# Local attention by quarter blocks of 32 queries, with the scores of three items in one piece on TensorE

## The chip, the cores and the metric

The kernel runs on one core of a Trainium2 chip. The time is device microseconds of that core for one launch. Before the change it is 918.82 us, the median of three runs (917.39 to 920.97).

## The reference, cut to what matters

Attention over 4 batches and 8 heads of width 64, then two feed-forward layers on the result. Each head has 32 global tokens and 512 local ones.

```python
window = 32
s_g = scale * np.matmul(q_g, k_all.transpose(0, 1, 3, 2))          # 32 global queries see all 544 keys
out_g = np.matmul(sm(s_g), v_all)
mask = np.abs(pos[:, None] - pos[None, :]) <= window               # a local query sees keys up to 32 away
s_ll = np.where(mask, scale * np.matmul(q_l, k_l.transpose(0, 1, 3, 2)), -1e9)
s_l = np.concatenate([scale * np.matmul(q_l, k_g.transpose(0, 1, 3, 2)), s_ll], axis=-1)   # and all 32 global keys
out_l = np.matmul(sm(s_l), np.concatenate([v_g, v_l], axis=2))
x = concat([out_g, out_l]).transpose(0, 2, 1, 3).reshape(B * S, H * D)     # 2176 tokens x 512
h = x @ w_in                                                       # 512 -> 2048
x = np.where(h >= 1, h, np.where(h <= -1, 0, (h + 1) ** 2 / 4)) @ w_out    # 2048 -> 512
return (x @ w_a * (x @ w_b)) @ w_out2                              # 512 -> 1536 -> 512
```

`sm` is a softmax over the last axis with the row maximum subtracted and 1e-9 added to the sum. All is float32; the weights arrive as float64 and are converted on the chip.

## The kernel before, in words

**Tiles.** The 16 blocks of 128 local queries and the block of global queries form six tiles of tokens (`TILES`, line 45): five of three blocks, 384 columns, and one of block 15 and the global block, 256 columns. The two layers work tile by tile. A unit of the first feed-forward layer (`h_unit`, line 767, and `x_unit`, line 796) takes 128 of the 2048 inner columns: 12 matmuls into a bank `hp`, the activation on ScalarE and VectorE, and 12 matmuls into four banks `acc`. Each product of the layers is three matmuls in the float32r format (`mm3`, line 438: high by high, low by high, high by low). After about 460 us the second layer follows; it has no attention in it.

**Attention.** An item (`Local`) is one block of 128 queries and one pair of heads; the two heads lie in the upper and lower 64 partitions. It is split into halves of 64 queries, each with 160 keys: a window of 128 and the 32 global ones. `s_pe` makes the scores with four float32 matmuls on 64x64 tiles of the array, into one bank a head. `s_post` adds the mask and takes the row's extreme in one VectorE instruction a head (line 193), then the exponential and its row sum on ScalarE (line 197). `norm` divides. `t_pe` and `t_post` transpose 320 columns in three overlapping transposes of 128 and copy the result to SBUF. `v_pe` runs once for a group, the items of a tile with one pair of heads (three, in tile 5 one): per item and head one matmul of 128 columns for the global keys and two of 64 columns for the halves, float32, on 128x64 tiles. `Glob` does the same for the global queries of one batch and four heads.

**Order.** `att_atoms` (line 351) is a generator that cuts this work into pieces. In step k it makes the scores of item k, normalises item k-1, transposes item k-2, and, when item k-3 ends a group, makes that group's products; scores and products then form one piece (`joined`). So a group of three has six pieces: three transposes, two scores, one of scores with products. Tile 0's pieces run first, alone, with a step of weight conversion (`W1.step`) after each eight. Then the pieces of tile t+1 are spread evenly over the `h_unit`s and `x_unit`s of the layer on tile t (`credit`, lines 863 to 910): tile 1 over tile 0's first six units, tile 2 over 26 units, tiles 3 and 4 over 16 each, tile 5 with the global items over the first 14 of tile 4. During the units of tiles 0 and 1 the float64 weights are converted: a raw tile of 512 KB lands (two buffers), line 105 on ScalarE and 106, 107 on VectorE make float32 of it, 114 and 115 split it in high and low. `paced` puts such a step behind the activation of the unit just issued.

The framework turns this into one fixed list for each engine. It plans by the order of the program, but takes an instruction ahead when an earlier one isn't ready by its estimate: in the trace the first matmuls of `hp` start at 31.02 us, ahead of tile 0's last transposes at 32.00. It also inserts all waits. PSUM has eight banks in two sets of four. In the set `h` lie scores, `hp` and, from tile 1 on, transposes and results; in the set `acc` the four accumulators and, for tile 0, transposes and results. DMAs are issued almost all from SP's queue, in order.

Of the kernel before, what the change touches and what calls it, by code (L numbers as in the profile page):

```python
# [9 lines left out]
F32 = mybir.dt.float32  # L10
# [8 lines left out]
P = 128  # L19
# [7 lines left out]
HQ = P // 2  # L27
KW = HQ + 2 * WIN + SG
QK = P + 2 * KW
C_ROW = (0, 2 * KW - P, KW - HQ)  # L30
# [18 lines left out]
NWARM, WARM_ITEMS = 2, 12  # L49
NCOLD = 3  # L50
FA = 6
START_ATOMS = 8
# [11 lines left out]
EBUFS = 3  # L64
PTBUFS = 3
VBUFS = 4


def body(tc, qk, vw, kg, vg, w1i, w1o, w2a, w2b, w2o, mask, eye, out):
# [13 lines left out]
    masks = ap.tile([P, 3, SG + KW], BF16, name="masks", bufs=1)  # L83
# [67 lines left out]
    class Local:  # L151
        def __init__(self, t, j, blk, p):
            self.t, self.j, self.p = t, j, p
            self.tag = "h" if t else "acc"
            self.blk = blk
            self.b, self.i = divmod(blk, SL // P)

        def load(self):
            n = nat["n"]
            nat["n"] += 1  # L160
            if 4 <= n < 4 + EARLY:
                self.qk = mp.tile([P, QK], F32, name="qk", tag="g", bufs=3)
            else:
                self.qk = gp["k"].tile([P, QK], F32, name="qk", tag="qk", bufs=4)
# [3 lines left out]
        def load_v(self):  # L168
            self.v = ap.tile([P, 3, P], F32, name="v", bufs=VBUFS)
            nc.sync.dma_start(self.v, vw[self.blk, self.p])  # L170

        def s_pe(self):
            self.s = [ps.tile([P, KW], F32, name=f"s{h}", tag="h") for h in range(2)]
            for a in range(2):
                for h in range(2):
                    r = slice(64 * h, 64 * h + 64)
                    c = slice(HQ * a, HQ * a + HQ)
                    nc.tensor.matmul(self.s[h][c], self.qk[r, c], self.qk[r, P + KW * a:P + KW * (a + 1)],
                                     start=True, stop=True, tile_position=(64 * h, HQ * a))

        def fill(self):
            w = ps.tile([P, 512], F32, name="warm", tag="acc")
            for _ in range(NWARM):
                nc.tensor.matmul(w[:, :P], ident, ident, start=True, stop=True)

        def s_post(self):
            m = 1 if self.i == 0 else (2 if self.i == SL // P - 1 else 0)
            self.ef = ap.tile([P, 2 * KW], F32, name="e", tag="e", bufs=EBUFS)
            self.e = self.ef.rearrange("p (h k) -> p h k", k=KW)
            mn = ap.tile([P, 2], F32, name="mn", tag="mn", bufs=EBUFS)  # L190
# [1013 lines left out]
```

## Time and profile before

| | before |
|---|---|
| median of 3 runs | 918.82 us (917.39 to 920.97) |
| the profiled execution | 920.25 us, its span 918.4 us |
| TensorE busy, granted clock | 904.6 us (98%), 1.000 |
| VectorE busy | 643.0 us (70%) |
| ScalarE busy | 508.5 us (55%) |
| DMA | 153.32 MB, mean 167 GB/s |

The span runs from the first to the last instruction. A busy TensorE is not TensorE at its peak, as its matmuls overlap in the record; what a piece costs is read from how far it moves the matmuls behind it. The granted clock of 1.000 is the upper of its two levels, 2.4 GHz.

### The profile page before, as it was taken

Reading aid. Unit: us, or ns where it says so; the run is one execution under the profiler, and the core shown is the slowest. Engines: PE = TensorE matmul, PEld = TensorE weight load, DVE = VectorE, ACT = ScalarE, POOL = GpSimd, SP = SyncE. Lnnn points to the kernel's source line nnn. Section 1 sums busy time; section 2 is a strip of 40 time slices with the busy share of each in tenths; the row PEclk is TensorE's granted clock in tenths of the full one; section 3 lists DMA queues with packets and bytes.
Section 4 is the critical chain, followed back from the end, with each engine's and each line's share of the span. In section 5 each row is a group of like instructions: output and inputs, shape, how many; then the busy total and the mean of one; then the engine's idle time right before and its main releaser. Section 6 shows DMA issues by size and latency. Waiting matters only on the chain.

```text
span 918.4 us, 17966 instructions
## 1 busy us (share of the span) xinstructions
PE 904.6 (98%) x6606; PEld 832.5 (91%) x6606; DVE 643.0 (70%) x1648; ACT 508.5 (55%) x1227; POOL 0.3 (0%) x5
## 2 busy tenths in 40 slices
PE   9999999999999999999999999999999999999998
PEld 6778998999999999887899999999998999999998
DVE  5888897676556555644478787777887658766683
ACT  7978675555455555534446465554655546555442
POOL 0000000000000000000000000000000000000000
PEclk9999999999999999999999999999999999999999
DMA  8986665765443444344354364443598530643431
GB/s 273 313 240 209 194 223 187 245 198 166 144 138 125 160 126 130 109 124 155 108 195 136 95 207 162 160 142 110 189 307 284 184 93 23 187 158 121 170 135 53
DMA packets 82025, 153.32 MB, mean 167 GB/s; under 512 B 9360, under 2 KB 48400, under 8 KB 81936
## 3 DMA queue, kind: packets, MB, share of 16 engines
q1 hardware_dynamic: 81360, 151.49, 51.1%
q8 instruction: 52, 0.85, 0.4%
q10 hardware_dynamic: 576, 0.67, 0.2%
q14 instruction: 37, 0.30, 0.1%
HBM read 118.83 MB, written 33.29 MB: 166 GB/s over the span
## 4 chain that ended last, share of the span: by engine, by line
PE 81%; DMA 9%; DVE 6%; ACT 2%; issue 1%; SPq 0%; ACTq 0%; DVEq 0%
PE acc L439 6%; PE hp L439 6%; PE hp L441 5%; PE acc L440 5%; PE acc L441 5%; PE hp L440 5%; PE pb L639 4%; PE pb L641 4%; PE pb L642 4%; PE py L706 3%; PE px L639 3%; PE px L641 3%; PE px L642 3%; PE py L707 3%; PE py L705 3%; DMA wraw<-in_w1o_dram 3%
## 5 line engine op out<-in xcount | busy, mean ns | idle before, releaser
L439 PE MATMUL hp<-xh,w 128*128 128x384 f32 (+1 forms) x384 | 130.8, 341 | 2.7 <-DVE m L787 1.6
L439 PE MATMUL acc<-g,w 128*128 128x384 f32 (+1 forms) x384 | 131.1, 341 | 0.0
L440 PE MATMUL acc<-g,w 128*128 128x384 f32 (+1 forms) x384 | 126.8, 330 | 0.0
L441 PE MATMUL acc<-g,w 128*128 128x384 f32 (+1 forms) x384 | 126.1, 328 | 0.0
L441 PE MATMUL hp<-xl,w 128*128 128x384 f32 (+1 forms) x384 | 125.9, 328 | 0.0
L440 PE MATMUL hp<-xh,w 128*128 128x384 f32 (+1 forms) x384 | 125.5, 327 | 0.0
L787 DVE SCALAR_TENSOR_TENSOR m<-hp,r 128x384 f32<-128x384 f32 (+1 forms) x96 | 51.2, 534 | 100.5 <-ACT r L786 100.3
L786 ACT ACTIVATE r<-hp,half 128x384 f32<-128x384 f32 (+1 forms) x96 | 53.8, 560 | 71.3 <-PE hp L441 69.6
L639 PE MATMUL pb<-w 128*128 128x384 f32 (+1 forms) x240 | 78.1, 325 | 1.5 <-DVE m L683 0.8
L439 PEld LDWEIGHTS hp<-xh,w 128*128 128x128 f32 x384 | 72.4, 188 | 7.3 <-DVE m L787 1.7
L114 ACT ACTIVATE w<-wt 128x512 fp32r<-128x512 f32 (+1 forms) x94 | 53.8, 572 | 45.1 <-PE pb L642 28.0
L641 PE MATMUL pb<-w 128*128 128x384 f32 (+1 forms) x240 | 78.2, 326 | 0.0
L642 PE MATMUL pb<-w 128*128 128x384 f32 (+1 forms) x240 | 78.0, 325 | 0.0
L439 PEld LDWEIGHTS acc<-g,w 128*128 128x128 f32 x384 | 72.4, 188 | 5.3 <-issue 4.3
L440 PEld LDWEIGHTS acc<-g,w 128*128 128x128 f32 x384 | 72.6, 189 | 1.4 <-issue 1.3
L441 PEld LDWEIGHTS hp<-xl,w 128*128 128x128 f32 x384 | 72.3, 188 | 1.0 <-DMA xl<-x0d 0.6
L441 PEld LDWEIGHTS acc<-g,w 128*128 128x128 f32 x384 | 72.4, 189 | 0.3 <-issue 0.2
L440 PEld LDWEIGHTS hp<-xh,w 128*128 128x128 f32 x384 | 72.5, 189 | 0.0
L791 ACT ACTIVATE g<-m 128x384 fp32r<-128x384 f32 (+1 forms) x96 | 48.3, 503 | 42.4 <-DVE m L788 42.1
L197 ACT ACTIVATE e<-e,mn 128x160 f32<-128x160 f32 x128 | 53.7, 421 | 26.6 <-DVE mn L193 26.6
L792 DVE TENSOR_TENSOR g<-m,g 128x384 fp32r<-128x384 f32 (+1 forms) x96 | 51.2, 533 | 20.1 <-ACT g L791 19.9
L115 DVE TENSOR_TENSOR w<-wt,w 128x512 fp32r<-128x512 f32 (+1 forms) x94 | 57.9, 616 | 2.7 <-ACT w L114 1.6
(168 smaller groups left out, 2133.1 us busy)
## 6 DMA issues: line engine op xcount, KB each, us to landing
qk<-in_qk_dram SPq DMA_DIRECT2D x62, 224.0 KB, 3.6
wt<-wd SPq DMA_DIRECT2D x50, 256.0 KB, 2.9
v<-in_vw_dram SPq DMA_DIRECT2D x64, 192.0 KB, 4.2
wraw<-in_w1i_dram SPq DMA_DIRECT2D x16, 512.0 KB, 4.3
wraw<-in_w1o_dram SPq DMA_DIRECT2D x16, 512.0 KB, 4.4
wraw<-in_w2a_dram SPq DMA_DIRECT2D x12, 512.0 KB, 3.9
wraw<-in_w2b_dram SPq DMA_DIRECT2D x12, 512.0 KB, 4.0
wd<-wt SPq DMA_DIRECT2D x24, 256.0 KB, 2.1
```

The lines of the kernel that those rows point to most:

```text
L114: nc.scalar.activation(hi, src, AF.Copy)
L115: nc.vector.tensor_tensor(lo, src, f32(hi), ALU.subtract)
L197: nc.scalar.activation(self.e[:, h], self.e[:, h], AF.Exp, bias=mn[:, h:h + 1], scale=-1.0, accum_out=self.sm[:, h:h + 1])
L439: nc.tensor.matmul(acc, whi, xhi, start=first, stop=False)
L440: nc.tensor.matmul(acc, wlo, xhi, start=False, stop=False)
L441: nc.tensor.matmul(acc, whi, xlo, start=False, stop=last)
L639: nc.tensor.matmul(out[:, :n], w[:, 0, r], hi[:, c, :n], start=start and c == 0, stop=False, skip_group_check=True)
L641: nc.tensor.matmul(out[:, :n], w[:, 1, r], hi[:, c, :n], start=False, stop=False, skip_group_check=True)
L642: nc.tensor.matmul(out[:, :n], w[:, 0, r], lo[:, c, :n], start=False, stop=k in (1, 5, 6) and c == 1, skip_group_check=True)
L786: at["act"] = nc.scalar.activation(r[:, :W], hp[:, :W], AF.Relu, bias=half, scale=0.5 / W_UP).ins
L787: nc.vector.scalar_tensor_tensor(m[:, :W], hp[:, :W], 1.0 / W_UP, r[:, :W], ALU.mult, ALU.max)
L792: nc.vector.tensor_tensor(gl[:, :W], m[:, :W], f32(gh[:, :W]), ALU.subtract)
```

## The change

An item is split into quarters of 32 queries, each with 128 keys. For that the keys of a block are laid out as seven slots of 32: the keys from 32 before the block to 64 into it, the 32 global keys, and the keys from 64 in the block to 32 behind it (`SLOTS`). Quarter a uses the four slots from a on; each such run holds its window of 96 and the global keys. Scores are then eight matmuls of 128 columns on 64x32 tiles, two transposes take the place of three, and the products are eight matmuls of 32 columns an item, each with 128 values of its own, on 128x64 tiles. Per item the queries and keys take 176 KB (224 before) and the values 256 KB (192 before).

The pieces are made anew. `groups` holds lists of items: three, or in tile 5 two; the global items count as groups of one. A group's scores are one piece, together with the products of the group two before it; ahead of it the group between is normalised. Each item's transposes are one piece. A group of three so has four pieces instead of six, 16 a tile instead of 24. Loads are asked for in each piece, at most one of each kind, as far as buffers allow (five tiles each). In tile 0 the row sum moves from ScalarE's exponential to one VectorE sum a group, three pieces have four fill matmuls each (nine had two each before), and a step of weight conversion comes after each five pieces. Result banks of tile 0 stay in `acc`.

```diff
-HQ = P // 2
-KW = HQ + 2 * WIN + SG
-QK = P + 2 * KW
+NQ = P // WIN
+SLOTS = (0, 1, 2, None, 3, 4, 5)
+QK = P + WIN * len(SLOTS)
-NWARM, WARM_ITEMS = 2, 12
-NCOLD = 3
+NWARM = 4
+START_GROUPS = 4
+EARLY_END = 13
-START_ATOMS = 8
+START_ATOMS = 5
-EBUFS = 3
+QKBUFS = 5
+EBUFS = 2
-VBUFS = 4
+VBUFS = 5
...
         def s_pe(self):
-            self.s = [ps.tile([P, KW], F32, name=f"s{h}", tag="h") for h in range(2)]
-            for a in range(2):
-                for h in range(2):
...
+            self.s = [ps.tile([P, self.nt, P], F32, name=f"s{h}", tag="h") for h in range(2)]
+            for n, it in enumerate(self.items):
+                for a in range(NQ):
                     for h in range(2):
                         r = slice(64 * h, 64 * h + 64)
+                        c = slice(WIN * a, WIN * a + WIN)
+                        nc.tensor.matmul(self.s[h][c, n], it.qk[r, c], it.qk[r, P + WIN * a:2 * P + WIN * a],
+                                         start=True, stop=True, tile_position=(64 * h, WIN * a))
+
+        def s_post(self):
...
+            for n, it in enumerate(self.items):
+                m = 1 if it.i == 0 else (2 if it.i == SL // P - 1 else 0)
+                for h in range(2):
+                    nc.vector.tensor_tensor_reduce(
+                        self.e[:, n, h], self.s[h][:, n], masks[:, m], -SCALE, 3.0e38, ALU.add, ALU.min,
+                        mn[:, n, h:h + 1])
+                for h in range(2):
+                    acc = self.sm[:, n, h:h + 1] if self.t else None
+                    nc.scalar.activation(self.e[:, n, h], self.e[:, n, h], AF.Exp, bias=mn[:, n, h:h + 1],
+                                         scale=-1.0, accum_out=acc)
+
+        def norm(self):
+            sm = self.sm[:, :self.nt]
+            if not self.t:
+                nc.vector.tensor_reduce(sm, self.e[:, :self.nt], mybir.AxisListType.X, ALU.add)
+            nc.vector.tensor_scalar_add(sm, sm, 1e-9)
+            nc.vector.reciprocal(sm, sm)
+            for n in range(self.nt):
+                nc.scalar.activation(self.e[:, n, 0], self.e[:, n, 0], AF.Copy, scale=self.sm[:, n, 0:1])
+                nc.vector.tensor_scalar_mul(self.e[:, n, 1], self.e[:, n, 1], self.sm[:, n, 1:2])
+
+        def t_pe(self, n):
+            it = self.items[n]
+            tp = ps.tile([P, 2, P], F32, name="tp", tag=self.tag)
+            for h in range(2):
+                nc.tensor.transpose(tp[:, h], self.e[:, n, h], ident)
+            it.pt = ap.tile([P, 2, P], F32, name="pt", tag="pt", bufs=PTBUFS)
+            nc.scalar.activation(it.pt, tp, AF.Copy)
+
+        def v_pe(self):
+            self.o = ps.tile([P, self.nt * P], F32, name="o", tag=self.tag)
+            for n, it in enumerate(self.items):
+                for a in range(NQ):
+                    for h in range(2):
+                        r = slice(64 * h, 64 * h + 64)
+                        q0 = WIN * a
+                        nc.tensor.matmul(self.o[r, n * P + q0:n * P + q0 + WIN], it.v[:, a, r],
+                                         it.pt[:, h, q0:q0 + WIN], start=True, stop=True)
...
+    def may_k():
+        n = ld["k"]
...
+        return n < ld["s_done"] + (8 if n < EARLY_END else QKBUFS)
...
+    def loads(first):
+        for may, fn in ((may_k, load_k), (may_v, load_v)):
+            k = 0
+            while may() and (k < 1 or (first and fn is load_k)):
+                fn()
+                k += 1
...
+    def piece(gs, gv):
+        def run():
+            loads(gs == 0)
+            if gs is not None:
+                if gs > START_GROUPS:
+                    groups[gs - 1].norm()
+                s_part(groups[gs])
+            if gv is not None:
+                v_part(groups[gv])
+            if 0 < (gs or 0) < START_GROUPS:
+                fill()
+            if gv is not None:
+                groups[gv].v_post()
+                if groups[gv].t == 0:
+                    x_chunk(0, groups[gv].items[0].p, widths(0))
+            if gs is not None:
+                groups[gs].s_post()
+        return run
+
+    def tpose(g, n):
+        def run():
+            loads(False)
+            if n == 0 and (g < START_GROUPS or g == len(groups) - 1):
+                groups[g].norm()
+            groups[g].t_pe(n)
+        return run
+
+    atoms = [piece(0, None), piece(1, None)]
     ends = {}
+    ns = 2
+    for g, grp in enumerate(groups):
+        n = grp.nt if isinstance(grp, Local) else 1
+        atoms += [tpose(g, i) for i in range(n)]
+        hold = g == START_GROUPS - 2
+        atoms.append(piece(None if hold or ns >= len(groups) else ns, g))
+        ns += not hold
+        if grp.t >= 0:
+            ends[grp.t] = len(atoms)
+        if g == START_GROUPS - 1:
+            atoms.append(piece(ns, None))
+            ns += 1
...
-                    n_atoms = sum(2 + it.last - joined(k + 3) for k, it in enumerate(todo, done["n"]))
+                    n_atoms = ends[goal[si]] - done["n"]
                     rate = n_atoms / (2.0 * (GLOB_END if t == nt - 2 else n_units) - 1)
```

For the global items the values load into the same buffers as the local ones, their last 32 rows as a tile of their own, and the copy of their transposes is two instructions instead of one.

## Rows read from the trace of the kernel before

**Rows 1.** Stretches: busy us of PE, PEld, DVE, ACT, POOL; clock, DMA, GB/s.

```profile
4.00:31.10 27.10, 25.69 (x298) 18.52 (x298) 19.36 (x102) 23.28 (x82) 0.00 (x0) 1.00 0.91 301
31.10:85.00 53.90, 50.31 (x468) 40.46 (x469) 46.23 (x164) 44.46 (x129) 0.00 (x0) 1.00 0.83 261
85.00:160.00 75.00, 73.00 (x511) 68.30 (x509) 63.84 (x157) 50.74 (x114) 0.00 (x0) 1.00 0.61 194
160.00:380.00 220.00, 219.92 (x1689) 203.72 (x1689) 134.17 (x403) 116.42 (x298) 0.00 (x0) 1.00 0.49 157
```

**Rows 2.** Chain of waits, 37:67 us: by line, then pieces (start, us).

```profile
by line: DMA wraw<-in_w1i_dram 63.0%; DVE wt L107 10.6%; ACT wt L105 8.0%; issue 6.8%; DVE w L115 4.4%; ACT w L114 2.1%; DVE m L788 1.8%; DVE wt L106 1.7%; DVE xl L330 1.6%; DVE sm L202 0.5%; DVE sm L201 0.3%; SPq L97 0.2%; DVE xraw L232 0.
...
38.05 5.60 DMA wraw<-in_w1i_dram
45.94 3.72 DMA wraw<-in_w1i_dram
```

**Rows 3.** Chain of waits, 85 to 150 us, by line.

```profile
by line: DMA wraw<-in_w1o_dram 39.3%; DVE wt L107 12.5%; ACT wt L105 6.3%; DVE wt L106 6.1%; DVE w L115 6.0%; DVE m L787 5.1%; DVE m L788 3.7%; issue 3.5%; DVE g L792 3.3%; PE hp L439 2.3%; ACT w L114 1.8%; DVE e L193 1.8%; PE hp L440 1.6%;
```

**Rows 4.** Chain of waits, 165 to 380 us, by line.

```profile
by line: PE acc L439 14.7%; PE hp L439 14.6%; PE hp L440 13.5%; PE hp L441 13.4%; PE acc L441 13.4%; PE acc L440 13.3%; PE s L178 5.8%; PE tp L209 4.3%; PE o L221 3.8%; PE o L227 3.2%
```

**Rows 5.** TensorE timeline round a scores piece: start us, us, what.

```profile
222.18 0.33 PE L440 MATMUL acc<-g,w 128*128 128x384 f32 x1
222.36 0.34 PE L441 MATMUL acc<-g,w 128*128 128x384 f32 x1
222.62 0.50 PE L178 MATMUL s<-qk 64*64 64x160 f32 x8
...
223.34 0.34 PE L440 MATMUL hp<-xh,w 128*128 128x384 f32 x1
```

**Rows 6.** TensorE's timeline behind a transposing piece.

```profile
225.28 0.49 PE L209 MATMUL tp<-ident,e 128*128 128x128 f32 x3
...
225.78 0.34 PE L440 MATMUL acc<-g,w 128*128 128x384 f32 x1
```

**Rows 7.** TensorE's timeline round a piece of scores and products.

```profile
354.42 0.34 PE L441 MATMUL acc<-g,w 128*128 128x384 f32 x1
354.69 0.50 PE L178 MATMUL s<-qk 64*64 64x160 f32 x8
355.12 0.44 PE L221 MATMUL o<-pt,v 128*64 128x128 f32 x4
355.39 0.40 PE L227 MATMUL o<-pt,v 128*64 128x64 f32 x8
355.62 0.39 PE L221 MATMUL o<-pt,v 128*64 128x128 f32 x4
...
356.08 0.39 PE L221 MATMUL o<-pt,v 128*64 128x128 f32 x4
...
356.63 0.45 PE L439 MATMUL hp<-xh,w 128*128 128x384 f32 x1
356.91 0.34 PE L440 MATMUL hp<-xh,w 128*128 128x384 f32 x1
```

**Rows 8.** TensorE's timeline, a global item's scores, then products.

```profile
388.60 1.12 PE L261 MATMUL sg<-kg 64*32 64x272 f32 x16
389.65 0.44 PE L221 MATMUL o<-pt,v 128*64 128x128 f32 x4
```

**Rows 9.** ScalarE's groups, 4 to 31.1 us: count, busy us, mean ns, idle before.

```profile
L197 ACT ACTIVATION_READ_ACCUMULATOR e<-e,mn 128x1 f32 x26 | 4.9, 189 | 0.0
L213 ACT ACTIVATE pt<-tp 128x384 f32<-128x384 f32 x10 | 4.8, 478 | 0.6 <-PE tp L209 0.6
```

**Rows 10.** VectorE's groups, 380 to 460 us.

```profile
L271 DVE TENSOR_REDUCE mng<-sg 128x1 f32<-128x272 f32 x16 | 6.8, 435 | 1.8 <-PE sg L261 1.6
```

**Rows 11.** VectorE's groups, 4 to 31.1 us.

```profile
L193 DVE CUSTOM_DVE_ANT_0 e<-s,masks 128x160 f32<-128x160 f32 x27 | 7.8, 320 | 9.0 <-PE s L178 5.0 <-PE tp L209 2.0 <-ACT pt L213 1.7
```

More of the change, by code (lines that the diff above doesn't have):

```diff
@@ L168, in load_v @@
         def load_v(self):
[L169 removed]
+            self.v = ap.tile([P, NQ, P], F32, name="v", tag="v", bufs=VBUFS)
             nc.sync.dma_start(self.v, vw[self.blk, self.p])
[L172 to L179 removed]
@@ L181, in fill @@
[L181 to L190, printed above, removed]
-            self.sm = ap.tile([P, 2], F32, name="sm", tag="sm", bufs=EBUFS)
-            for h in range(2):
-                nc.vector.tensor_tensor_reduce(
-                    self.e[:, h], self.s[h], masks[:, m, SG - SG * h:SG - SG * h + KW], -SCALE, 3.0e38,
-                    ALU.add, ALU.min, mn[:, h:h + 1])
-            for h in range(2):
-                nc.scalar.activation(self.e[:, h], self.e[:, h], AF.Exp, bias=mn[:, h:h + 1],
-                                     scale=-1.0, accum_out=self.sm[:, h:h + 1])
@@ L211, in t_post, with fill @@
[L211 to L223 removed]
+    def fill():
+        w = ps.tile([P, 512], F32, name="warm", tag="acc")
+        for _ in range(NWARM):
+            nc.tensor.matmul(w[:, :P], ident, ident, start=True, stop=True)
@@ L234, in body @@
+        def v_post(self):
+            runs = []
+            for n, it in enumerate(self.items):
+                if runs and runs[-1][0].p == it.p:
+                    runs[-1][2] += 1
+                else:
+                    runs.append([it, n, 1])
+            for it, n, w in runs:
+                nc.vector.tensor_copy(xraw_cur[self.t][it.p][:, it.j * P:(it.j + w) * P],
+                                      self.o[:, n * P:(n + w) * P])
     class Glob:
-        last = True
         t = -1
+        nt = 1
@@ L394, in body @@
-    att = att_atoms()
+    groups = []
+    for t, blks in enumerate(TILES):
+        loc = [(j, blk) for j, blk in enumerate(blks) if blk != GLOB]
+        its = [Item(j, blk, p) for p in range(NPAIR) for j, blk in loc]
+        n = len(loc) if len(loc) > 1 else 2
+        groups += [Local(t, its[i:i + n]) for i in range(0, len(its), n)]
+        for b in GSCHED.get(t, []):
+            groups += [Glob(b, q) for q in range(2)]
+    ld = {"k": 0, "v": 0, "s_done": 0, "v_done": 0, "vb": 0, "g": 0}
@@ new lines, in body, with load_k, load_v @@
+    flat_items = [(g, it) for g in groups for it in g.items]
+    first_glob = next(n for n, (g, it) in enumerate(flat_items) if isinstance(g, Glob))
+    started = set()
+    def load_k():
+        n = ld["k"]
+        g, it = flat_items[n]
+        it.load()
+        ld["k"] += 1
+        if n == 0:
+            nc.scalar.dma_start(masks, mask)
+        elif n == 3:
+            nc.scalar.dma_start(ident, eye)
+    def load_v():
+        g, it = flat_items[ld["v"]]
+        it.load_v()
+        ld["v"] += 1
+        ld["vb"] += 1 + isinstance(g, Glob)
```

231 lines of the change are left out of this document (88 added, 143 removed).

## The prediction

> **What bounds the kernel now.** I read the table of stretches first, to see where TensorE has slack, then the chain of waits of each stretch, to see what sets the pace there, then TensorE's timeline around single pieces of attention, for their prices, and last the groups of instructions of the start.
>
> The table of stretches [rows 1] shows four regimes. From 4 to 31 us tile 0's attention runs alone; ScalarE is busy 23.28 of 27.10 us. From 31 to 85 us tile 1's attention runs beside six units of the first layer and the conversion of their weights; TensorE, VectorE and ScalarE are busy for 82 to 93%. From 160 to 380 us TensorE is busy 219.92 of 220.00 us, VectorE 134.17. The chains say what that means. From 37 to 67 us 63% of the chain is the landing of a weight tile, 3.7 to 5.6 us each, then conversion, then the next tile into the freed buffer [rows 2]: TensorE isn't the bound there. From 85 to 150 us the same loop and VectorE's part of it hold most of the chain and matmuls are a small part [rows 3]. From 165 to 380 us the chain is all TensorE [rows 4]: there a microsecond of TensorE is a microsecond of the kernel, and all of what follows after 460 us is only shifted.
>
> **What a group of three items costs TensorE now.** One main matmul starts 0.17 us after the other [rows 5]. A transposing piece moves the second main matmul behind it from 225.28 + 0.17 to 225.78 [rows 6]: 0.33 us for three transposes, 0.11 each, with no cost at the borders. A scores piece on its own: from 222.36 to 223.34, less two main matmuls, 0.63 us [rows 5]. A scores piece with the products of a group: from 354.42 to 356.91, less two, 2.14 us [rows 7]. A group has three of the first, two of the second, one of the third: 0.99 + 1.26 + 2.14 = 4.39 us.
>
> **The change, part by part.** *Transposes:* two for three, 3 x 0.22 = 0.66 us; saves 0.33.
>
> *Scores:* three items in one piece, so two of three entries and exits go. What stands: 0.27 us from the last main matmul to the first score [rows 7], and 0.28 us at the end from the first main matmul to the second [rows 7]. Between them the passes (a float32 matmul leaves two records, one a pass; the eight records of a scores piece lie within 0.50 us [rows 5], so matmuls on different tiles of the array run side by side, and eight records are two passes). Two passes of 160 columns with what surrounds them take 0.43 us [rows 7], four of 272 columns 1.05 us [rows 8]; the difference, 0.62 us for 768 columns, is 0.81 ns a column, and 0.17 us is left for entry and drain. Six passes of 128 columns: 0.62 + 0.17 = 0.79 us. This takes eight tiles of 64x32 to run together; the trace has four of them [rows 8] and four of 64x64, which fill the array [rows 5]. If only four ran at once it would be 1.41 us. I take 0.79, because the whole array is in use there [rows 5].
>
> *Products:* the columns that stream for an item fall from 2 x 128 + 4 x 64 to 8 x 32, the two heads side by side. But each of the 24 passes (3 items, 4 quarters, 2) loads its own 128x64 weights. Before, four passes of 64 columns take 0.23 us (355.39 to 355.62) [rows 7], 0.057 each. No row has a pass of 32 columns. Below, half of that, 0.029, if the product alone counts; above, 0.086, if the load and the product follow each other. I take 0.057, the nearest row: the first pair of passes after the switch takes 0.27 us where a later pair takes about 0.23 (0.46 from 355.62 to 356.08 less 0.23), so 0.04 us is a bare weight load, more than 32 columns would hide. Then 24 x 0.057 = 1.37, with 1.51 - 3 x 0.46 = 0.13 around it [rows 7]: 1.50 us, against 1.51 now. The halved columns buy nothing.
>
> Two rules of the Trainium skill part here. "TensorE: Matmul & The Clock Gate", section LDWEIGHTS, has a load take P/1.2 ns for P columns whatever the rows: 53 ns for these 64, and the products stay at 1.50 us; the 0.04 and 0.057 us above agree with it. "TensorEngine Tiling (Array Packing)", section Instruction Overhead, has a matmul of few columns cost about 60 cycles, 25 ns as an estimate: by that alone a group's products take some 0.7 us. No run here shows a 32-column pass yet; the second is the first rival below.
>
> The piece: 0.27 + 0.79 + 1.50 + 0.28 - 0.35 = 2.49 us; the group 0.66 + 2.49 = 3.15 us; 1.24 us saved in each group, nearly all from borders and transposes.
>
> *Where it counts.* (a) Tiles 3 and 4 and the second half of tile 2, after 150 us, ten groups: 12.4 us. (b) Tile 5's four single items become two groups of two; by the same prices (two transposing pieces of 0.22 and 0.27 + 0.58 + 1.04 + 0.28 - 0.35 = 1.82 a group, against four items at 0.33 + 0.43 + 0.59 and borders, some of them shared with the global items) about 1.5 us. (c) Tile 2's first two groups lie beside the weight loop [rows 3]: between 0 and 2.5, I take 1.2. (d) Tile 1's four groups: up to 5.0, but for half of that stretch the weight loop sets the pace [rows 2] and none of it is touched; I take 2.5. (e) The start. 24 reads of the accumulator, 0.19 us each [rows 9], go, as tile 0 now sums on VectorE; the copy of transposes shrinks from 384 columns to 256. Both together relieve ScalarE by up to 7 us. Against this VectorE gets a sum over 768 elements a group: 272 elements take 0.435 us [rows 10], so at most 1.2 us, 4.9 for four groups. It has 7.7 us free [rows 1]. The first reductions now also wait for three items' loads, and 12 fill matmuls stand where 18 did: the granted clock of the start is 1.00, 2.4 GHz [rows 1], and some us at 1.2 GHz would cost as many. So from -2 to +7; I take 3.
>
> *Edits that I cost at nothing.* Masking, exponentials and normalisation of 128 columns instead of 160 on engines that are off the path after 160 us (VectorE has 86 us free there [rows 1]); in the early stretches their relief, some 0.3 us an item, is inside (c) to (e). Bytes: 176 KB + 256 KB an item for 224 + 192; 4% more on a DMA that is 49% busy after 160 us and 83 to 91% before 85 us [rows 1]; there it can lengthen the landings of weight tiles [rows 2], inside the bounds of (d) and (e). Loads move from fixed steps to each small step, at most one of each kind a step; they queue on SP beside the weight tiles, and with five buffers of each kind a group's three tiles are asked for one to three steps ahead. The global items keep their matmuls; their copy becomes two. Two buffers for the exponentials instead of three hold a group each, so two groups live where three items did.
>
> Sum: 12.4 + 1.5 + 1.2 + 2.5 + 3 = 20.6 us. The profiled execution took 920.25 us, 1.85 outside the span: it would become 899.7. It is 0.16% above the median of the runs, 918.82, so the predicted median is 898.2 us. What is late next is the weight loop before 150 us, and TensorE still after it.
>
> **Rivals.** *First: the products' passes do shorten* to 0.029 us. For it: the load overlaps the running product in every row. Against: the bare load of 0.04 us. It would take 24 x 0.028 = 0.67 us more off each group, eight or so more for (a) and (b): 890.
>
> *Second: the load and the product of a short pass follow each other*, 0.086 us. For it: no row has a load longer than its product. Against: passes of 64 columns run at the length of their product. 0.70 us back per group: 906.
>
> *Third: the early stretches give nothing* because the weight loop carries on as it is and the start trades ScalarE's relief for VectorE's sums and for waits in a batch of three. For it: the loop's share of the chains [rows 2, 3]. Against: ScalarE's 86% in the start [rows 1]. (c) to (e) fall away: 905. The eight tiles running four at a time, so that the change doesn't do what it says, adds 0.62 us to each group and lands there too, 906.
>
> *Fourth, slower: the scores hold their banks.* Scores, transposes, results and the first layer's sums share four banks of PSUM. A group now keeps two until VectorE has gone through six reductions, 0.32 us each now [rows 11], 1.9 us, in a queue with everything else. Where VectorE has 39% free (160 to 380 us [rows 1]) they may take 4.9 us. Cover is the products, 1.5 us, and one unit of 12 main matmuls, 2.1 us. The rest, 1.3 us in 12 pieces, is 15.6; before 160 us, with VectorE 85% busy, say 3 us in six pieces, 18: 918.8 - 20.6 + 33.6 = 932. It decides from 20.6/18 = 1.15 us a piece. Against it: the reductions of an item need no more than its scores and can run under the products.
>
> **Chances.** The forecast 0.58, in a range of its own from 892 to 905; first rival 0.12; second 0.10; third 0.15; fourth 0.05. The range of 8 in 10 takes the two middle rivals in and most of the first: 888 to 908. Half a per cent (4.6 us) is about what a measurement can tell from no change: faster by over that 0.92, within it 0.04 (the second and third rival together, or a mild fourth), slower 0.04.
>
> **What would show it.** In the profile after, a transposing piece moves the main matmul by 0.22 us; a joint piece costs 2.5 us, its 48 product records a row of 1.4 us and its scores 0.6 to 0.8; from 160 us the chain is still TensorE alone, and VectorE's idle time isn't seen ahead of its matmuls. The last stage, after the attention, keeps its 458 us. The forecast is wrong if the joint piece is far from 2.5 us, if first-layer matmuls wait for VectorE after 160 us, or if the first of them starts later than 31 us.

## The result and the profile after

The changed kernel takes 905.95 us, median of four runs (905.32 to 906.93), against 919.89 us in four runs of the kernel before (917.39 to 923.74): a ratio of 0.985 (95% interval 0.981 to 0.988). The forecast was 898.2 us with a range of 888 to 908, so the time lies inside the range and 7.75 us above the forecast. The profiled execution took 905.32 us, with a span of 903.5 us.

| | before | after |
|---|---|---|
| span of the profiled execution | 918.4 us | 903.5 us |
| TensorE busy | 904.6 us | 887.1 us |
| mean granted clock | 1.000 | 0.987 |
| VectorE, ScalarE busy | 643.0, 508.5 us | 634.3, 489.1 us |

The clock is the line to stop at. The first fence is the page's row of the granted clock of the kernel after, 40 slices of 22.6 us; before, all 40 digits were 9.

```profile
PEclk8799999999999999999999999999999999999999
```

The table of stretches of the same execution shows where: the same four stretches as [rows 1], with the same columns.

```profile
4.00:31.10 27.10, 23.27 (x384) 17.09 (x384) 15.48 (x76) 15.77 (x46) 0.00 (x0) 0.81 0.78 254
31.10:85.00 53.90, 48.13 (x637) 40.11 (x635) 44.07 (x149) 42.29 (x132) 0.00 (x0) 0.87 0.82 269
85.00:160.00 75.00, 74.78 (x635) 72.87 (x635) 66.58 (x169) 53.57 (x131) 0.00 (x0) 1.00 0.69 216
160.00:380.00 220.00, 219.69 (x2097) 212.28 (x2097) 133.47 (x375) 112.33 (x304) 0.00 (x0) 1.00 0.49 158
```

In the start ScalarE and VectorE are busy for 15.8 and 15.5 us of 27.1, where they were for 23.3 and 19.4: over the whole stretch neither of them is the bound any more. But the granted clock is 0.81 and 0.87 up to 85 us, and 1.00 behind it. Cut finer, it has only the two levels:

```profile
10.00:14.00 4.00, 1.24 (x49) 0.78 (x48) 2.75 (x9) 1.45 (x5) 0.00 (x0) 1.00 1.00 379
14.00:24.25 10.25, 10.13 (x133) 7.52 (x117) 4.93 (x21) 5.78 (x16) 0.00 (x0) 0.50 0.55 165
24.25:34.50 10.25, 9.30 (x182) 7.07 (x180) 8.11 (x30) 7.76 (x21) 0.00 (x0) 1.00 0.79 257
34.50:48.10 13.60, 11.95 (x90) 10.02 (x90) 7.13 (x29) 7.89 (x26) 0.00 (x0) 0.50 0.80 278
48.10:85.00 36.90, 33.73 (x482) 28.17 (x481) 33.54 (x114) 31.92 (x101) 0.00 (x0) 1.00 0.82 269
```

For 10.25 + 13.60 = 23.85 us TensorE runs at 1.2 GHz, and it is busy for 10.13 + 11.95 = 22.08 us of them. If that work took half as long at 2.4 GHz, 11.0 us would be saved; that is the most that the lower level can have cost here. Ahead of the first fall TensorE worked 1.24 us in 4.

TensorE's timeline of the kernel after shows what it waited for (start, us, what; in brackets the idle time before it and what ended it):

```profile
10.11 0.86 PE L190 MATMUL s<-qk 64*32 64x128 f32 x32
13.73 0.51 PE L190 MATMUL s<-qk 64*32 64x128 f32 x16 [2.76 <-DMA qk<-in_qk_dram]
14.17 0.69 PE L222 MATMUL tp<-ident,e 128*128 128x128 f32 x2
...
31.41 1.59 PE L233 MATMUL o<-pt,v 128*64 128x32 f32 x48
...
34.43 0.67 PE L500 MATMUL hp<-xh,w 128*128 128x384 f32 x1 [0.86 <-ACT xh L340]
...
37.38 1.54 PE L222 MATMUL tp<-ident,e 128*128 128x128 f32 x6 [1.65 <-ACT e L215]
38.85 2.78 PE L233 MATMUL o<-pt,v 128*64 128x32 f32 x48
...
43.70 0.52 PE L500 MATMUL hp<-xh,w 128*128 128x384 f32 x1
44.02 0.52 PE L501 MATMUL hp<-xh,w 128*128 128x384 f32 x1
```

At 10.11 us the scores of group 2 start; two items go through, and the third waits 2.76 us for its load. The transposes of group 0 stand behind it in TensorE's fixed order. The second fall, at 34.5 us, has a wait of 0.86 us ahead of it and one of 1.65 us inside it. The price of the lower level can be read in two places: the 48 product records of a group take 1.59 us at 31.41 and 2.78 us at 38.85, 1.75 times as long; and one main matmul starts 0.32 us after the other (43.70, 44.02) instead of 0.17 [rows 5], 1.85 times. By these factors the 22.08 us hold 9.5 to 10.1 us more than at 2.4 GHz, an estimate.

A second reading is when the k-th main matmul starts (the matmuls of the first layer, counted in the traces from zero). It is the same work in both kernels, so differences between columns are what each stretch gained:

| k | 0 | 72 | 144 | 432 | 1520 | 1900 | end |
|---|---|---|---|---|---|---|---|
| before, us | 31.0 | 55.6 | 83.5 | 144.2 | 379.3 | 475.7 | 918.4 |
| after, less before | -2.3 | +9.5 | +5.6 | +1.5 | -10.6 | -15.6 | -14.9 |

The start loses 9.5 us up to the 72nd, and every stretch behind it up to the 1900th gains: 3.9, 4.1, 12.1 and 5.0 us. The loss isn't the clock alone. Here is all that stands ahead of the 72nd main matmul, first before the change, then after it, with the columns of [rows 1]:

```profile
0.00:55.57 55.57, 51.23 (x512) 39.75 (x512) 40.74 (x174) 44.43 (x135) 0.30 (x5) 1.00 0.88 287
0.00:65.06 65.06, 55.38 (x737) 43.62 (x737) 41.61 (x165) 41.68 (x123) 0.30 (x5) 0.82 0.76 250
```

TensorE stands idle for 9.7 us instead of 4.3, 5.3 more. The lower clock makes its work 9.5 to 11.0 us longer (the estimates above), and what is left over, 5.3 to 6.8 us, is work that fell away. One place of the waiting is the 2.76 us above. Another shows in the chain of waits:

```profile
27.85 0.56 DVE xraw L244
...
36.94 0.40 ACT e L215
37.38 1.54 PE tp L222 x6
```

From 27.85 to 36.94 us it runs over VectorE, busy for 9.04 of these 9.09 us, where normalisation, one of the new row sums (0.86 us), copies, the next scores' reductions and weight conversion stand in one queue, then over ScalarE; the granted clock there is 1.00 up to 34.5 us.

The first layer itself runs to 530.5 us before the change and to 514.9 after it, so the second layer doesn't follow at about 460 us, as the description of the kernel before has it: what ends there (459.0 us) is the attention.

In the steady stretch the pieces can be read as in [rows 6, 7]: first a transposing piece, then a group's scores with the products, both between main matmuls.

```profile
340.63 0.34 PE L502 MATMUL acc<-g,w 128*128 128x384 f32 x1
340.80 0.38 PE L222 MATMUL tp<-ident,e 128*128 128x128 f32 x2
...
341.20 0.34 PE L501 MATMUL hp<-xh,w 128*128 128x384 f32 x1
```

```profile
224.98 0.34 PE L502 MATMUL acc<-g,w 128*128 128x384 f32 x1
225.25 0.94 PE L190 MATMUL s<-qk 64*32 64x128 f32 x48
226.12 1.59 PE L233 MATMUL o<-pt,v 128*64 128x32 f32 x48
227.64 0.44 PE L500 MATMUL hp<-xh,w 128*128 128x384 f32 x1
227.92 0.34 PE L501 MATMUL hp<-xh,w 128*128 128x384 f32 x1
```

From 340.63 to 341.20 less two main matmuls of 0.173 is 0.22 us. From 224.98 to 227.92 less two is 2.59 us, 0.87 of it from the first score to the first product and 1.52 for the products. A group is 3 x 0.22 + 2.59 = 3.26 us. The chain of waits from 165 to 380 us is TensorE alone, as in [rows 4]:

```profile
by line: PE hp L500 15.0%; PE hp L501 14.2%; PE hp L502 14.1%; PE acc L500 14.0%; PE acc L502 13.9%; PE acc L501 13.9%; PE o L233 7.6%; PE s L190 3.8%; PE tp L222 3.0%; PE sg L273 0.5%
```

### The profile page after: what moved, and what is told of

The parts are those of the page before. It is cut to its first block, busy times and chain, and to the rows that moved or that the text cites. A ratio compares the mean times of both kernels' runs of the same rounds, so it can differ in the third digit from the quotient of the medians.

```text
span 903.5 us, 19267 instructions
## 1 busy us (share of the span) xinstructions
PE 887.1 (98%) x7298; PEld 834.1 (92%) x7298; DVE 634.3 (70%) x1587; ACT 489.1 (54%) x1192; POOL 0.3 (0%) x5
## 4 chain that ended last, share of the span: by engine, by line
PE 91%; DMA 4%; DVE 3%; ACT 2%; issue 1%; ACTq 0%; SPq 0%; DVEq 0%
PE hp L500 7%; PE acc L500 7%; PE hp L502 7%; PE acc L501 7%; PE hp L501 7%; PE acc L502 7%; PE pb L700 4%; PE pb L702 4%; PE pb L703 4%; PE o L233 4%; PE py L767 3%; PE px L700 3%; PE py L768 3%; PE px L702 3%; PE px L703 3%; PE py L766 3%
## 5 line engine op out<-in xcount | busy, mean ns | idle before, releaser
L500 PE MATMUL hp<-xh,w 128*128 128x384 f32 (+1 forms) x384 | 132.7, 346 | 1.4 <-ACT xh L340 0.9
L500 PE MATMUL acc<-g,w 128*128 128x384 f32 (+1 forms) x384 | 127.5, 332 | 1.7 <-ACT g L852 1.7
L501 PE MATMUL hp<-xh,w 128*128 128x384 f32 (+1 forms) x384 | 126.9, 330 | 0.0
L501 PE MATMUL acc<-g,w 128*128 128x384 f32 (+1 forms) x384 | 125.7, 327 | 0.0
L502 PE MATMUL acc<-g,w 128*128 128x384 f32 (+1 forms) x384 | 125.2, 328 | 0.0
L853 DVE TENSOR_TENSOR g<-m,g 128x384 fp32r<-128x384 f32 (+1 forms) x96 | 51.1, 533 | 22.6 <-ACT g L852 22.4
L205 ACT ACTIVATE e<-e,mn 128x128 f32<-128x128 f32 x128 | 48.2, 390 | 14.8 <-DVE mn L200 14.5
```

The lines of the kernel that those rows point to most:

```text
L500: nc.tensor.matmul(acc, whi, xhi, start=first, stop=False)
L501: nc.tensor.matmul(acc, wlo, xhi, start=False, stop=False)
L502: nc.tensor.matmul(acc, whi, xlo, start=False, stop=last)
L853: nc.vector.tensor_tensor(gl[:, :W], m[:, :W], f32(gh[:, :W]), ALU.subtract)
```

## The experiments

Theory: the steady part came as priced, and the start lost its gain to TensorE's clock, which fell behind a wait in a fixed order. Rivals: the start is late because three items wait for each other, whatever the clock; and, for the steady part, that the gain is the narrower blocks' alone.

Each time is the median with its range, beside runs of the kernel before on the same chip. The chips differ between experiments; the medians of the kernel before on them are 919.64 to 920.77 us.

**More filling products (e1_fill14).**

```
-NWARM = 4
+NWARM = 14
```

> The changed kernel with 14 filling products behind each of the second to fourth piece instead of 4, so that TensorE has work beside its two early waits (2.76 us before the third item of group 2's scores, 1.65 us before the first transposes). Clock theory (the start is lost because the granted clock stands at 1.2 GHz for 10.25 + 13.6 us): the granted clock is 2.4 GHz from about 10 us on, the 72nd main matmul starts about 9 us earlier than in the changed kernel, 897 us (894 to 900). Rival (the start is lost because a group's scores wait for three loads and a group's norm for six exponentials): the clock comes back but the first main matmuls stay late, 904 to 907 us. Second rival (the added fills themselves, 30 x 0.11 us = 3.3 us, stand on the path): 901 to 903 us.

903.06 us (898.61 to 904.83), ratio 0.980 (0.978 to 0.983); the profiled run took 898.61 us. Its timeline in the start:

```profile
7.00 3.39 PE L174 MATMUL warm<-ident 128*128 128x128 f32 x28
10.32 0.63 PE L190 MATMUL s<-qk 64*32 64x128 f32 x20
10.88 0.87 PE L222 MATMUL tp<-ident,e 128*128 128x128 f32 x6
11.68 0.43 PE L190 MATMUL s<-qk 64*32 64x128 f32 x12
13.43 0.45 PE L190 MATMUL s<-qk 64*32 64x128 f32 x16 [1.31 <-DMA qk<-in_qk_dram]
13.81 1.12 PE L233 MATMUL o<-pt,v 128*64 128x32 f32 x32
```

The edit did two things at once: with longer fills the order worked out for TensorE has the transposes of group 0 ahead of the late load, so the wait is 1.31 us instead of 2.76. The granted clock is 1.00 up to 47 us (then 0.50 for 7 us), the 72nd main matmul starts 7.4 us earlier than in the changed kernel, where 9 were expected, and the end comes 6.7 us earlier. The profiled run lies in the clock theory's range (894 to 900 us), the median just above the second rival's (901 to 903 us). The four other runs have mean clocks of 0.992 to 0.998, against 0.985 to 0.989 in the changed kernel. So the clock came back for the most part, and the fills stand on the path as well; the run doesn't tell the shares. The fills' price in the expectation was wrong: a fill leaves two records, and 14 take 3.39 us, 0.242 each and not 0.11.

**The ninth load earlier (e6_early_qk), and both edits (e7_early_qk_fill14).** The first has one line more, so that the second piece, with its loads, stands ahead of the first weight loads; the second has 14 fills as well.

```
 att_step(10 ** 9)
+att_step(10 ** 9)
 W1.load_to(sp["raw"])
```

> The changed kernel with the first two W1 loads issued behind the second piece instead of ahead of it, so that the ninth qk load (issued at 7.06 us, landed at 13.69 us) no longer stands behind 2 x 512 KB on SP's queue; fills stay at 4. If the one long wait of TensorE (2.76 us at 11 us) is what takes the clock down, it is gone here without any added work: clock at 2.4 GHz at least to the second wait at 34 us, time about 899 to 902 us, less what the later W1 loads cost. If that wait only ends early and the clock falls all the same, 904 us or more.

902.47 us (901.08 to 904.95), ratio 0.981 (0.980 to 0.983). The wait didn't go, it moved to the next item. Timeline, then stretches:

```profile
10.34 0.44 PE L222 MATMUL tp<-ident,e 128*128 128x128 f32 x2 [0.57 <-ACT e L215]
14.83 0.60 PE L190 MATMUL s<-qk 64*32 64x128 f32 x2 [4.05 <-DMA qk<-in_qk_dram]
15.37 1.11 PE L222 MATMUL tp<-ident,e 128*128 128x128 f32 x4
```

```profile
4.00:11.75 7.75, 4.89 (x154) 2.95 (x154) 5.80 (x33) 4.93 (x16) 0.00 (x0) 1.00 1.00 334
11.75:25.25 13.50, 10.42 (x136) 8.06 (x136) 5.31 (x24) 6.69 (x19) 0.00 (x0) 0.50 0.65 209
```

Two records of the following group's scores now stand between the transposes and wait 4.05 us for their own load; DMA is full up to there (share 1.00). The clock falls for 13.5 us, and later three times for 3.4 us (at 39.0, 56.1 and 144.8 us). So this run didn't test what it was made for: the wait was there, and with it the fall. It is 3.5 us faster than the changed kernel all the same, between its two expected ranges; the 13.6 us at half clock from 34.5 us are gone in it.

> Both edits: the ninth qk load ahead of the W1 loads and 14 fills. Clock theory: 2.4 GHz throughout as with 14 fills alone, and the wait of 2.8 us gone; 895 to 898 us if the transposes of group 0 were behind that wait, equal to 14 fills alone (897) if W1's loads bound the start (they land later here by what the qk load takes).

899.32 us (897.96 to 903.58), ratio 0.979 (0.977 to 0.981). The profiled run has 1.2 GHz for some 3.4 us only, from 15.1 us; its 72nd main matmul starts 0.7 us earlier than in the kernel before. The median is 1.3 us above the expected range, the profiled run (898.10 us) at its edge.

**The kernel before without its fills (e2_before_nofill).**

```
-NWARM, WARM_ITEMS = 2, 12
+NWARM, WARM_ITEMS = 0, 12
```

> The kernel before without its fills (0 instead of 2 behind each of nine items). Clock theory: TensorE's early idle time is no longer filled, the granted clock falls to 1.2 GHz in part of 10 to 45 us, the 72nd main matmul comes 5 to 10 us later, 924 to 930 us. Rival (fills only take TensorE's time, 18 x 0.11 = 2 us): 917 to 920 us with the clock at 2.4 GHz.

925.28 us (924.35 to 927.36), ratio 1.006 (1.005 to 1.007). The clock did fall:

```profile
12.00:18.75 6.75, 5.75 (x48) 4.18 (x49) 1.75 (x13) 2.44 (x8) 0.00 (x0) 0.50 0.62 195
18.75:22.50 3.75, 2.62 (x20) 1.27 (x18) 3.49 (x13) 3.31 (x12) 0.00 (x0) 0.95 0.71 195
22.50:25.75 3.25, 3.25 (x38) 2.65 (x38) 1.34 (x8) 2.04 (x9) 0.00 (x0) 0.53 0.91 244
```

The 72nd main matmul came 3.0 us later, less than the 5 to 10 expected, and the loss stayed about the same from there on (4.1 us in the span). But one of its six runs had a mean granted clock of 1.000 and took 925.25 us. The other five, at 0.991 to 0.994, took 924.35 to 927.36 us. So in this kernel the clock can't be shown to cost anything: without fills the order worked out for TensorE differs too. What the loss comes from was not separated.

**Quarter blocks alone (e4_quarters_alone).** Keys, masks, transposes and products of the change; the order, the fills and the pieces of one item as before.

```
-            for a in range(2):
+            for a in range(NQ):
...
-                    c = slice(HQ * a, HQ * a + HQ)
-                    nc.tensor.matmul(self.s[h][c], self.qk[r, c], self.qk[r, P + KW * a:P + KW * (a + 1)],
-                                     start=True, stop=True, tile_position=(64 * h, HQ * a))
+                    c = slice(WIN * a, WIN * a + WIN)
+                    nc.tensor.matmul(self.s[h][c], self.qk[r, c], self.qk[r, P + WIN * a:2 * P + WIN * a],
+                                     start=True, stop=True, tile_position=(64 * h, WIN * a))
...
```

> The kernel before with quarter blocks of 32 queries and their own 128 keys (its data layout, scores, masks, two transposes, eight product passes), but with the old order: each item's scores as a piece of their own, fills as before, the third joined with the older group's products. By the prediction's prices a group costs .66 transposes + 2 x .58 scores alone + 2.09 joint = 3.91 us instead of 4.39, so from the 432nd to the 1520th main matmul (ten groups, 235.1 us before, 223.0 after) 230.3 us, and as the old fills stay, the granted clock stays at 2.4 GHz in the start; 911 to 914 us in all. Rival A (the narrower blocks bring the whole gain): 223 us between those matmuls, about 906 us. Rival B (nothing without the grouping, since eight short passes cost what six longer ones did): 235 us, 918 us or more.

From the 432nd to the 1520th main matmul 230.6 us, against 230.3 expected: both rivals are out. In all 914.68 us (911.00 to 916.83), ratio 0.993 (0.990 to 0.996). That the clock stays at 2.4 GHz was wrong: it fell for some 10 us from 13.8 us, behind a wait of 1.91 us for the load of an item's values, which are larger now (256 KB for 192). So a fall needs no batch of three. The four runs are one kernel in one order at different clocks: the one with a mean clock of 1.000 took 911.00 us, those at 0.991 to 0.994 took 914.24 to 916.83 us, 3.2 to 5.8 us more. A third item's scores and the products stand like this:

```profile
307.12 0.45 PE L177 MATMUL s<-qk 64*32 64x128 f32 x16
307.50 1.59 PE L221 MATMUL o<-pt,v 128*64 128x32 f32 x48
309.02 0.44 PE L435 MATMUL hp<-xh,w 128*128 128x384 f32 x1
```

Products: 307.50 to 309.02, 1.52 us, as in the changed kernel.

**Grouping alone (e3_groups_alone).** The changed kernel with the keys and products of the kernel before.

```
-                for a in range(NQ):
+                for h in range(2):
+                    r = slice(64 * h, 64 * h + 64)
+                    nc.tensor.matmul(self.o[r, n * P:(n + 1) * P], it.v[:, 2, r], it.pt[:, 2], start=True, stop=False,
+                                     skip_group_check=True)
+                for a in range(2):
...
```

> The other part alone: half blocks of 64 queries with 160 keys and their separate pass over the global keys as before, but a group's three scores in one piece with the older group's products, and the changed kernel's order of the start (one qk and one v buffer fewer than the changed kernel, and one buffer fewer for converted weights in the start, for room in SBUF; so only the stretch behind the start is read). By the prediction's prices a group costs .99 + 2.66 = 3.65 us, so 227.7 us from the 432nd to the 1520th main matmul. If the two parts add, .74 here and .48 with quarter blocks alone make the 1.24 of the prediction (1.13 measured). Rival (switching between scores and other passes costs nothing once pieces are queued, so grouping brings nothing): 235 us. In the start the clock falls as in the changed kernel, since its fills and waits are the same.

227.4 us between the same matmuls, against 227.7. With 4.5 us from quarter blocks alone and 7.7 from grouping alone the two parts make 12.2 us; the change has 12.1. They add. (In all 909.70 us, one run; not compared, for its fewer buffers.) What was expected of the start didn't come: behind a wait of 1.96 us for a load the clock fell for 3.4 us only (at 15.9 us, and twice more, at 53.5 and 77.4 us), and the 72nd main matmul starts 3.9 us later than before the change, not 9.5.

**Products of 64 columns (e5_stream64).** The first three quarters of an item stream twice the columns.

```
+                        q1 = min(q0 + 2 * WIN, P)
-                        nc.tensor.matmul(self.o[r, n * P + q0:n * P + q0 + WIN], it.v[:, a, r],
-                                         it.pt[:, h, q0:q0 + WIN], start=True, stop=True)
+                        nc.tensor.matmul(self.o[r, n * P + q0:n * P + q1], it.v[:, a, r],
+                                         it.pt[:, h, q0:q1], start=True, stop=True)
```

> The changed kernel with the products of the first three quarters of an item streaming 64 columns instead of 32 (the surplus columns are overwritten by the next quarter's pass). If the pass is bound by loading its 64 columns of values (what the trace of the changed kernel seems to show: 0.057 us for 32 columns as for 64 before), product passes stay at 0.057 us, the joint piece at 2.59 us and 223 us from the 432nd to the 1520th main matmul. If a pass's time follows its columns (the first rival of the prediction, 0.027 us for 32 columns more), 18 x 0.027 = 0.5 us more a group and 228 us.

904.06 us, one run. The joint piece:

```profile
303.80 0.34 PE L503 MATMUL acc<-g,w 128*128 128x384 f32 x1
304.07 0.94 PE L190 MATMUL s<-qk 64*32 64x128 f32 x48
304.94 1.59 PE L234 MATMUL o<-pt,v 128*64 128x64 f32 x48
306.46 0.44 PE L501 MATMUL hp<-xh,w 128*128 128x384 f32 x1
306.74 0.34 PE L502 MATMUL hp<-xh,w 128*128 128x384 f32 x1
```

1.52 us from the first product to the main matmul behind, and 2.59 for the piece: the same as with 32 columns. Between the 432nd and the 1520th main matmul 223.8 us, where 228 would have been the rival's. So what a pass streams, 32 or 64 columns, doesn't bound it. Nor does the number of instructions: the scores in the same piece leave as many records, 48, in 0.87 us. Loading the 64 columns of values is the reading that is left over; it isn't shown, as no run changed the number of columns loaded, and a fixed price of a pass would look the same.

**How many fills, and where (e8, e11, e9, e12).** All have the ninth load earlier; they differ from the run with both edits in the fills. e8 has 20 three times, e9 has 10 three times, e11 has 14 behind the second and third piece only, e12 has 14 behind the second and 7 behind the third.

```
-            if 0 < (gs or 0) < START_GROUPS:
+            if 0 < (gs or 0) < START_GROUPS - 1:
                 fill()
```

(That is e11, beside its 14 fills; e8 and e9 change the number alone, and e12 gives each piece its own.)

> The ninth qk load ahead of the W1 loads and 20 fills instead of 14 (with which TensorE still stood 1.49 us before 13.87 us, and 3.4 us of half clock followed). Clock theory: 2.4 GHz from about 10 us to the end in the profiled run, 895 to 898 us, and less spread over the runs than with 14 (897.96 to 903.58). Rival (18 fills more x 0.11 = 2 us stand on the path): 899 to 901 us at full clock.

900.63 us (899.85 to 905.17), ratio 0.978 (0.976 to 0.980): the rival's time. Two runs with a mean clock of 1.000 took 899.85 and 900.14 us, so more fills cost time at full clock. The rival had priced 18 more at 0.11 us; at the 0.242 us measured they are 4.4 us, of which the median shows 1.3 against 14 fills. The profiled run was the slowest, 905.17 us: its clock fell for 3.4 us at 15.8 us, and again, in the second layer, at 691.6 us, behind a wait of 1.9 us for ScalarE.

> The ninth qk load ahead of the W1 loads and 14 fills behind the second and third piece, none behind the fourth. In the run with 14 fills three times they took 3.39, 4.37 and 3.39 us of TensorE (0.242 us each at 2.4 GHz), and TensorE then went from the third fill to the first main matmul at 33.26 us with hardly a wait, so they stood on the path there. If the clock holds without the third, the first main matmul comes 2 to 3 us earlier and the time is 895 to 897 us; if the transposes behind it wait for ScalarE as long, 898 to 899 us as with three; if the clock falls again behind 24 us, 900 to 903 us.

896.57 us (894.29 to 899.99), ratio 0.975 (0.972 to 0.977), the best of all. The first main matmul starts at 24.8 us, more than 8 us earlier than with three fills, as the order changes again; the 72nd only 2.1 us earlier than there. Its stretches:

```profile
4.00:31.10 27.10, 23.98 (x502) 19.36 (x505) 21.20 (x99) 20.32 (x62) 0.00 (x0) 1.00 0.97 324
31.10:85.00 53.90, 50.44 (x651) 44.10 (x652) 47.20 (x159) 45.43 (x144) 0.00 (x0) 0.97 0.89 285
```

Against [rows 1] ScalarE is busy for 20.3 us of the start instead of 23.3, VectorE for 21.2 instead of 19.4, and the clock is at 1.00 there. Some 3.4 us at 1.2 GHz remain, from 38.4 us.

> The ninth qk load ahead of the W1 loads and 10 fills three times, 2.9 us less of TensorE than with 14; the planned order then has a first transpose pair and a tenth item's scores behind group 2, and that item's load is late as with 4 fills (4.05 us of waiting there). Clock theory: the clock falls at about 12 to 16 us, 900 to 904 us. Rival (the number of fills alone decides, and 10 are enough): 896 to 898 us.

900.36 us (899.53 to 901.00), ratio 0.978 (0.976 to 0.980), as the clock theory had it:

```profile
10.00:13.25 3.25, 0.81 (x31) 0.38 (x18) 1.75 (x6) 1.89 (x5) 0.00 (x0) 1.00 0.98 376
13.25:23.50 10.25, 9.26 (x74) 8.04 (x74) 4.77 (x20) 4.03 (x12) 0.00 (x0) 0.50 0.60 208
```

More fills than the changed kernel, but in an order that has a late load between the transposes: a wait of 3.43 us, and 10.25 us at 1.2 GHz. So the number of fills alone doesn't keep the clock in this place; the waits in TensorE's order matter too. In the runs whose wait there was 2.76, 4.05 and 3.43 us (changed kernel, e6, e9) the clock fell for 10.25 to 13.5 us; in those where it was 1.31 to 1.55 us (e1, e7, e11) it stayed up there or fell for 3.4 us. But the length of one wait orders the runs only roughly: 1.91 us (e4) brought some 10 us and 1.96 us (e3) 3.4 us, and of e7 and e11, with the same order up to 15 us and waits of 1.49 and 1.55 us, only e7's clock fell. The second fall of the changed kernel, 13.60 us from 34.5 us, isn't in e9, and e9 is 5.6 us faster than the changed kernel with a first fall of the same length.

> The ninth qk load ahead of the W1 loads, 14 fills behind the second piece, 7 behind the third, none behind the fourth: between the kernels with 14 twice and with 4. If the clock holds, 1.7 us less of TensorE than with 14 twice, 894 to 897 us; if it falls, 900 us or more.

901.83 us (897.24 to 904.28), ratio 0.979 (0.977 to 0.982). Its clock fell for 6.8 us from 29.0 us and for 3.4 us from 42.7 us; the second of the two outcomes expected. Ahead of the fall at 29.0 us stands no long wait, but three short ones for loads of queries and keys, 0.39, 0.66 and 0.68 us within 5 us.

## Why the prediction was right, and where it was wrong

**What bounds the kernel, and that steady work pays in full: right.** From 160 to 380 us TensorE is busy 219.69 of 220 us, and the chain is TensorE alone.

**(a) Ten groups, 12.4 us: right.** 12.1 us between the 432nd and the 1520th main matmul. By the pieces a group costs 3.26 us instead of 3.15, so 1.13 saved and not 1.24, 11.3 for ten; the 0.8 us to 12.1 was not traced to a row. The miss of 0.1 us a group is the scores term: 0.87 us from the first score to the first product, against 0.79. That eight tiles of 64x32 run together is thereby shown: four at a time would have needed 1.41 us by the prediction's prices.

**Products stay at 1.50 us: right,** 1.52 for 24 passes, 0.063 each with what surrounds them. The first two rivals are out: short passes don't shorten, and 0.086 us a pass would have made 2.06 us. The rule of the Trainium skill in "TensorE: Matmul & The Clock Gate", section LDWEIGHTS, P/1.2 ns for a load (53 ns for 64 columns), fits this price. The Trainium skill's figure in "TensorEngine Tiling (Array Packing)", section Instruction Overhead, about 60 cycles for a short matmul (25 ns, an estimate), is not what a pass costs here.

**(b) Tile 5, 1.5 us: too small,** 5.0 us. The prediction priced the single items alone. What it left out is borders of the global items beside them: main matmuls stretched at the entry of such pieces lose 2.4 us less, counted over their gaps in the traces, and the global scores take 8.4 us instead of 10.3, where two gaps of 0.7 us are gone.

**(c) Tile 2's first two groups, 1.2 us: too small,** 4.1 us: two groups at 1.13, and a wait of 1.6 us of a first-layer matmul for VectorE (of the kernel before, from 85 to 150 us) that doesn't come back; a new one of 0.6 us for ScalarE stands against it. **(d) Tile 1, 2.5 us:** 3.9 us from the 72nd to the 144th, more than priced; but that is the second half of tile 1's attention, and what its first half gained or lost is inside the loss of the start.

**(e) The start, 3 us (-2 to +7): this is the step that failed.** It lost 9.5 us up to the 72nd main matmul. Of its reasons, VectorE's sum over 768 elements takes 0.946 us, four times 3.8, below the 4.9 allowed, and ScalarE is relieved: 20.3 us up to 31.1 us in e11, where the first layer is further on than before the change, against 23.3 (the 15.8 of the changed kernel also lack work that only came later). It also named the danger, first reductions waiting for three items' loads, fewer fills, and the same cost for some us at 1.2 GHz, and then took 2.4 GHz from the row of the kernel before. In its place stand 22.08 us of TensorE's work at 1.2 GHz, which is 9.5 to 11.0 us longer for it, and 5.3 us more of waiting. Without the clock's part the 72nd would start 0 to 1.5 us earlier than before, an estimate that takes all of that work to stand on the path; the run that comes nearest to it, e11, has it 2.8 us earlier. The bound of -2 allowed for some us at the lower clock, and not for 24. Nor did its sign of being wrong show it: the first main matmul starts at 28.7 us, ahead of the 31 us that were named, and the loss lies behind it.

So that the time lies inside the range is luck, two misses against each other: 9.5 us lost instead of 3 gained in the start, 12.5 too much, and 3.5 + 2.9 + 1.4 us more than priced in (b), (c) and (d), less 0.3 in (a) and 0.7 that the last stage gave back. The third rival (the early stretches give nothing, 905 us) has the right time and half the reason: the start does have its waits in a batch of three (2.76 us for the third item's load, 5.3 us more of waiting in all), but (c) and (d) gave 8 us, and it is the start with its clock that took them. The fourth (scores hold their banks) is out: from 160 to 380 us TensorE has one wait, 0.3 us for a DMA, and none for VectorE.

**What stays open.** The fills move the order of TensorE's work as well as its idle time; no edit changed one and left the other. That the clock costs time is shown best by e4, whose runs differ in nothing else on record; e2's runs show no such cost. How the 9.5 us divide between clock and waits is not settled: e5, which differs from the changed kernel in its products alone, has 17.1 us at half clock in place of 23.9, a wait of 2.40 us for ScalarE in place of 1.65, and starts its 72nd main matmul only 1.0 us earlier. Nor is the spread between runs of e7, e11 and e12 (5 to 7 us) explained beyond that their slower runs mostly show the lower mean clocks.

**A version that beats both:** e11, 896.57 us; its slowest run, 899.99 us, lies below the fastest of the changed kernel, 905.32 us, and its interval (0.972 to 0.977) below the changed kernel's (0.981 to 0.988).

## What to carry to other kernels

When a change makes batches larger in a stretch where TensorE isn't full, look in the fixed order for the first instruction that waits for the last load of a batch, and for what stands behind it: a wait of about 3 us there was followed by 10 us at half clock. More fills (e9) or an earlier load (e6) didn't take that fall away as long as a late load stood between the transposes, though both kernels are faster than the changed one (900.36 and 902.47 us); work that was ready, put ahead of the wait, did (e1, e11). And don't price a short pass by what it streams alone: halving the columns of a pass that loads 64 columns of weights gained nothing, doubling them again cost nothing.

## What the runs showed of the hardware

The long stretches at 1.2 GHz came while TensorE was busy for most of the time: 10.13 of 10.25 us in the changed kernel, 10.42 of 13.50 in e6, 9.26 of 10.25 in e9. So the clock doesn't come back as soon as there is work again. In the same three kernels DMA's share was 0.98 to 1.00 ahead of the fall and 0.55 to 0.65 during it: a reading that fits is that with TensorE at half speed the buffers come free later and the loads wait for them; no run tested it.
